# Attention, 2D-FFT mixing and an FFN on one core: VectorE's order tied to the first batch's transform, that transform by row chunks, W2's Gram products later, fewer unused products

## The chip, the cores and the metric
One core of one Trainium2 chip runs the program alone. The metric is the device time of one execution in microseconds (us). Every run of the kernel before gave between 1111.65 and 1112.94 us.

## What is computed
For each of 8 batches: windowed causal attention (8 heads, 576 positions, head size 64, window 128, a linear distance bias with a slope per head), its result `x` (576 x 512) mixed by a two-dimensional Fourier transform, normalised, and sent through a two-layer FFN. Cut to what matters:

```
scores = q @ k^T / 8 - slope[h] * (i - j)      where 0 <= i - j < 128
x      = softmax(scores) @ v                   # heads side by side: 576 x 512
u      = x + real(fft(fft(x, axis=seq), axis=model))
un     = (u - mean(u)) / sqrt(var(u) + 1e-6)
out    = u + relu(un @ W1) @ W2                # W1 512 x 2048, W2 2048 x 512
```

## The kernel before
**Pieces of work.** A batch's attention runs over four pairs of heads, numbered p = 4b + j. A pair has three groups of scores (`scores`, L370): q·k products on TensorE, a VectorE operation that adds the bias and reduces to the minimum (L399), ACT's exponential, then either a transpose on TensorE (`turn`, L423, batches 0 and 1, in f32) or f16 high and low parts and DMA transposes (`halves`, L406, the later batches). `values` (L435) multiplies by v, and `weigh` (L460) divides by the sums and writes the result into the tile X. In the trace an f32 product of scores or values shows as two records. After each group of scores of the first eight pairs, `busy` (L282) issues two 128x512 products whose result nobody reads.

**The transform** (`fourier`, L502) takes X in three chunks c of the sequence. `begin` (L505) clears one row. `fold_a`, `fold_b`, `fold_c`, `fold_d` (L513 to L557) add and subtract mirrored halves on VectorE and split them into f16 high (ACT) and low parts (VectorE). `rows(g)` (L559) multiplies the four column groups g by a cosine or sine table, nine products for each g over all three chunks; `rows_hi` (ACT) and `rows_lo` (VectorE) split the result. `cols(j)` (L591) is the second dimension, for three blocks of rows j; `cols_out` (ACT) brings it back, `cols_add` (VectorE) adds it to X: for j < 2 to X[j] and, mirrored, to X[2 + j]. `norm` (L656) takes two tiles: statistics (L669, L670), reciprocal deviation (L671 on VectorE, the power on GpSimd, L672), two scalings on ACT (L681, L682), a subtraction on VectorE (drawn at L155) and a DMA transpose on SP's queue into uT, which the FFN reads.

**The FFN** (`ffn`, L694): per two tiles, products with W1 (L707), relu on ACT (L712), its low part on VectorE (L155), products with W2 (L721), an addition, a store. Batches alternate 384 and 480 W1 products.

**The weights** (`weights`, L161) are made once, in 16 chunks of 512 columns: a load on SP's queue into one of four (W1) or three (W2) stages, `rebias` on ACT (L180), `join` on VectorE (L185, L186; the stage is then free), four Gram products on TensorE (`gram`, L192), from which `top_of` and `scale` take one scale; after it f16 high parts (`high`, ACT, L212) and low parts (`low`, VectorE, L215). W2's stages are the X buffers of batches not yet begun.

**What sets the order.** The program is written out by a list of times. `put(t, f)` (L151) pushes a piece of work with a time of the list, and the loop at L780 pops them in order; a framework then places instructions on each engine, with this order as their priority, by a model of when each is ready. On the chip every engine takes its instructions in that fixed order, SP's DMA queue too. Times of attention come from BEGIN and PACE, those of the transform from `put` calls at the end of `fourier` (L628 to L654), those of the FFN from FORWARD, those of the weights from the last lines (L778, L779).

## Time and profile before

| what | value |
|---|---|
| time, median of 3 runs | 1111.89 us (1111.65 to 1112.94) |
| profiled execution | 1110.7 us, span 1108.9 us |
| mean granted TensorE clock | 0.964 of full speed |
| TensorE busy | 1057.5 us, 95% |
| VectorE, ACT, GpSimd busy | 721.4, 570.1, 19.2 us |
| DMA share over the span (largest queue) | 34.2% |

Start times count from the span's first instruction. Products on TensorE are pipelined, so a busy time includes a tail that overlaps the next; where a price is wanted, the distance between starts is the better figure.

### The profile page before, as it was taken

Reading aid. Unit: us, or ns where it says so; the run is one execution under the profiler, and the core shown is the slowest. Engines: PE = TensorE matmul, PEld = TensorE weight load, DVE = VectorE, ACT = ScalarE, POOL = GpSimd, SP = SyncE. Lnnn points to the kernel's source line nnn. Section 1 sums busy time; section 2 is a strip of 40 time slices with the busy share of each in tenths; the row PEclk is TensorE's granted clock in tenths of the full one; section 3 lists DMA queues with packets and bytes.
Section 4 is the critical chain, followed back from the end, with each engine's and each line's share of the span. In section 5 each row is a group of like instructions: output and inputs, shape, how many; then the busy total and the mean of one; then the engine's idle time right before and its main releaser. Section 6 shows DMA issues by size and latency. Waiting matters only on the chain.

```text
span 1108.9 us, 23827 instructions
## 1 busy us (share of the span) xinstructions
PE 1057.5 (95%) x9252; PEld 739.8 (67%) x9252; DVE 721.4 (65%) x2255; ACT 570.1 (51%) x1330; POOL 19.2 (2%) x53
## 2 busy tenths in 40 slices
PE   7999898997999989999899999999999999999998
PEld 5776675765766657585658567675657667767665
DVE  4888689349768586979595868778575844362111
ACT  5887595337545376476654657375535531241000
POOL 0000000000000000000000000000000000000000
PEclk9995879998999999999899999999999999999999
DMA  9952042126432326335432364335422330020000
GB/s 359 362 170 65 13 92 68 49 48 123 104 83 54 95 56 139 88 74 117 103 89 60 70 111 95 77 70 100 113 77 40 68 70 1 20 48 20 20 11 20
DMA packets 178544, 95.35 MB, mean 86 GB/s; under 512 B 152960, under 2 KB 161152, under 8 KB 178432
## 3 DMA queue, kind: packets, MB, share of 16 engines
q1 hardware_dynamic: 177856, 92.39, 34.2%
q8 instruction: 72, 1.18, 0.4%
q10 hardware_dynamic: 576, 1.45, 0.3%
q14 instruction: 40, 0.33, 0.1%
HBM read 48.19 MB, written 9.44 MB: 52 GB/s over the span
## 4 chain that ended last, share of the span: by engine, by line
PE 67%; DVE 15%; DMA 7%; ACT 5%; issue 4%; SPq 1%; POOL 0%; DVEq 0%; ACTq 0%
PE fp L721 27%; PE fp L707 25%; PE sp L386 4%; PE pd L563 3%; DVE P L399 3%; DMA qr<-q_dram 3%; PE pv L447 2%; DMA pt<-P 2%; DVE P L155 2%; DVE hbuf L155 1%; DVE st L669 1%; PE sp L430 1%; DMA uT<-un 1%; ACT P L155 1%; DMA hbuf<-w_dram 1%
## 5 line engine op out<-in xcount | busy, mean ns | idle before, releaser
L721 PE MATMUL fp<-wall,hbuf 128*128 128x512 f16 x1728 | 391.5, 380 | 4.2 <-DVE hbuf L155 4.2
L707 PEld LDWEIGHTS <-wall 128*128 128x128 f16 x3840 | 343.7, 100 | 70.7 <-issue 14.1
L707 PE MATMUL fp<-uT,wall 128*128 128x256 f16 x3072 | 372.2, 278 | 17.1 <-DMA uT<-un 9.3
L721 PEld LDWEIGHTS <-hbuf 128*128 128x128 f16 x1728 | 164.0, 98 | 190.1 <-issue 7.9
L155 ACT ACTIVATE P<-P,nb 128x256 f32<-128x256 f32 x320 | 142.9, 479 | 78.3 <-DVE nb L399 76.4
L712 ACT ACTIVATE hbuf<-fp 128x512 f16<-128x512 f32 x144 | 84.8, 589 | 183.7 <-PE fp L707 183.4
L155 DVE SCALAR_TENSOR_TENSOR hbuf<-fp,hbuf 128x512 f16<-128x512 f32 x144 | 99.0, 688 | 113.3 <-ACT hbuf L712 112.4
L399 DVE CUSTOM_DVE_ANT_0 P<-sp,rg,nsl 128x256 f32<-128x256 f32 x240 | 98.4, 449 | 21.6 <-PE sp L386 11.0
L155 DVE SCALAR_TENSOR_TENSOR P<-P 128x256 f16<-128x256 f32 x240 | 88.7, 389 | 32.8 <-ACT P L412 31.7
L412 ACT ACTIVATE P<-P 128x256 f16<-128x256 f32 x240 | 86.5, 383 | 11.3 <-DMA pt<-P 5.0
L386 PE MATMUL sp<-kk,qq 64*128 64x256 f16 (+5 forms) x800 | 76.1, 280 | 2.2 <-ACT qq L361 1.2
L155 DVE SCALAR_TENSOR_TENSOR X<-fp,misc,X 128x512 f32<-128x512 f32 x32 | 23.7, 742 | 52.6 <-PE fp L721 52.6
L452 PE MATMUL pv<-vhs,pt 128*128 128x65 f16 x432 | 54.2, 195 | 0.3 <-DVE X L471 0.2
L455 PE MATMUL pv<-vl,pt 128*128 128x64 f16 x432 | 54.3, 193 | 0.0
L456 PE MATMUL pv<-vhs,pt 128*128 128x65 f16 x432 | 54.3, 194 | 0.0
L707 PE MATMUL fp<-wall,wall 128*128 128x128 f16 x768 | 47.5, 223 | 2.5 <-DVE hbuf L155 2.2
L452 PEld LDWEIGHTS <-pt 128*128 128x128 f16 x432 | 41.1, 98 | 8.4 <-issue 0.8
L455 PEld LDWEIGHTS <-pt 128*128 128x128 f16 x432 | 40.4, 99 | 7.8 <-issue 0.2
L386 PEld LDWEIGHTS <-qq 64*128 64x128 f16 (+1 forms) x720 | 30.8, 99 | 19.9 <-issue 14.8
L456 PEld LDWEIGHTS <-pt 128*128 128x128 f16 x432 | 40.5, 97 | 0.1
L563 PE MATMUL pd<-tab_sb,fh 128*128 128x289 f16 x174 | 39.7, 293 | 0.0
L546 ACT ACTIVATE fh<-abcd,sc 128x512 f16<-128x512 f32 (+1 forms) x24 | 17.3, 719 | 39.7 <-DVE abcd L538 39.7
(160 smaller groups left out, 1249.7 us busy)
## 6 DMA issues: line engine op xcount, KB each, us to landing
qr<-q_dram SPq DMA_DIRECT2D x28, 304.0 KB, 3.1
hbuf<-w_dram SPq DMA_DIRECT2D x16, 512.0 KB, 6.8
out_dram<-X SPq DMA_DIRECT2D x32, 256.0 KB, 2.2
vr<-v_dram SPq DMA_DIRECT2D x23, 320.0 KB, 3.1
kr<-k_dram SPq DMA_DIRECT2D x24, 289.0 KB, 3.0
X<-w_dram SPq DMA_DIRECT2D x11, 512.0 KB, 4.8
pt<-P SPq DMA_TRANSPOSE x240, 2.4
wall<-w_dram SPq DMA_DIRECT2D x5, 512.0 KB, 4.3
```

The costliest lines, as they stand in the source:

```text
L155: put(now[0] + dt, lambda: f(*a, **kw))
L386: T.matmul(sp[e][:m, col:col + n], qq[h, c0:c0 + m], keys(kk[h], ti), start=(x == 0), stop=(x == len(prods) - 1))
L399: V.tensor_tensor_reduce(pt[:m, 0:n], sp[e][:m, col:col + n], tab[:m, pc:pc + n], mul, 3.0e38, ALU.add, ALU.min, nb[:m, ti:ti + 1])
L412: A.activation(hi, P32, AF.Copy, scale=2.0 ** 14)
L447: T.matmul(pv[:, ti], pt[:, col:col + 128], ops[p][2][:, e, vc], start=first, stop=last)
L452: o = T.matmul(pv[:, ti], ph, vh[:, e, vc], start=first, stop=False)
L455: T.matmul(pv[:, ti, 0:D], ph, vl[:, e, vc], start=False, stop=False)
L456: T.matmul(pv[:, ti], pl, vh[:, e, vc], start=False, stop=last)
L563: T.matmul(zp[:, :NS], st["in", c][l][:m, g], tab1_sb[:m, (0 if g < 2 else 2) + t, c], start=(c == 0 and p == 0), stop=(c == 2 and p == 2))
L707: T.matmul(fp[:, i * n:(i + 1) * n], w1_ap(e, c, f0 + i), uT[:, j, c, 0:n], start=(c == 0 and p == 0), stop=(c == 3 and p == 2))
L712: A.activation(ht[:, 0], fp, AF.Relu)
L721: T.matmul(op, hh[f][:, a, i * 128:(i + 1) * 128], w2_ap(e, f), start=(f == 0 and p == 0), stop=(f == 15 and p == 2))
```

## The change
- `CHAIN = 0.15`; the first two times of FORWARD, at which the FFNs of batches 0 and 1 enter the list, go from 17.1 to 22 and from 39.6 to 41.6.
- `busy` issues its unused products for the first four pairs and not the first eight.
- W2's chunks are placed 0.4 instead of 0.5 apart, its high and low parts from 16.8 instead of 18.5, and all of its Gram products at one late time instead of one chunk behind each join.
- Batch 0's transform is no longer placed by times of its own: it is a list of steps, 0.15 apart. The row products go by chunk (`rows_of`: groups 0 to 2, chunk 2, then 0, then 1; group 3 whole), the mirrored addition into X[2 + j] is a step of its own, and the first two tiles are normalised before the third block of columns.
- While the list's time is below 25, every VectorE instruction gets an order dependency, without a semaphore, on the last VectorE instruction of that chain, so that VectorE's order is the list's there.
- `squares` of pairs above 9 is kept in program order, and it and the scales of those pairs are placed 0.6 or 0.7 later; the load of pair 8 is placed at 19.2.

```diff
+CHAIN = 0.15
...
-FORWARD = (17.1, 39.6, 64.7, 88.7, 112.7, 136.7, 160.7, 184.7, 208.7)
+FORWARD = (22, 41.6, 64.7, 88.7, 112.7, 136.7, 160.7, 184.7, 208.7)
...
+    def link(f, *a, **kw):
+        f(*a, **kw)
+        linked[0] = True
+
+    def place(b, t, f, *a, **kw):
+        if b == 0:
+            put(t, lambda: link(f, *a, **kw))
+        else:
+            put(t, lambda: f(*a, **kw))
...
-            put(t + 2 * dt - 0.3, gram, c)
+            put(t + 2 * dt - 0.3 if wi == 0 else t0 + 16.5 * dt, gram, c)
...
+        if p > 4 * NF + 1:
+            tc.keep_in_program_order(o)
...
-        for _ in range(SPIN if p < 8 else 0):
+        for _ in range(SPIN if p < 4 else 0):
...
+        def rows_of(gs, c):
+            for g in gs:
+                if c == 2:
+                    st["zp", g] = bank(b)
+                for p, (l, t) in enumerate(((0, 0), (1, 0), (0, 1))):
+                    T.matmul(st["zp", g][:, :NS], st["in", c][l][:KCH[c], g], tab1_sb[:KCH[c], (0 if g < 2 else 2) + t, c],
+                             start=(c == 2 and p == 0), stop=(c == 1 and p == 2))
...
+        if b == 0:
+            uTs[b] = []
+            pair = lambda i: lambda: st["X"][2 * i:2 * i + 2]
+            steps = [(begin, ), (fold_b, 2), (fold_c, 2), (fold_a, 0), (fold_b, 0), (fold_d, 2), (fold_c, 0),
+                     (rows_of, (0, 1, 2), 2), (fold_a, 1), (fold_b, 1), (fold_d, 0), (fold_c, 1), (rows_of, (0, 1, 2), 0),
+                     (fold_d, 1), (rows_of, (0, 1, 2), 1)]
+            for g in range(3):
+                steps += [(rows_hi, g), (rows_lo, g)]
+                if g == 0:
+                    steps += [(rows, 3)]
+            steps += [(rows_hi, 3), (rows_lo, 3), (middle, ), (middle_out, ), (cols, 1), (cols_out, 1), (cols, 0), (cols_add, 1), (mirrored, 1),
+                      (cols_out, 0), (cols_add, 0), (norm, b, pair(0), None), (cols, 2), (mirrored, 0), (cols_out, 2),
+                      (cols_add, 2), (norm, b, pair(1), None)]
+            for i, (g, *a) in enumerate(steps):
+                place(b, t0 + CHAIN * i, g, *a)
+            return
...
-            t0 -= 2.6 if p == 4 * NF else 2.9
+            t0 = 19.2 if p == 4 * NF else t0 - 2.9
...
-                put(t0 + 1.2 + 0.2 * x, squares, p, x)
+                put(t0 + (1.2 if late or p == 4 * NF else 1.8) + 0.2 * x, squares, p, x)
+            if p > 4 * NF + 1:
+                t0 += 0.7
...
-    weights(1, 9.5, 0.5, 18.5, 0.4)
+    weights(1, 9.5, 0.4, 16.8, 0.3)
+    traced, seen = nc.cur_bb.bb.instructions, 0
+    tied = {mybir.EngineType.DVE}
     while queue:
         now[0], _, f, a = heappop(queue)
+        linked[0] = False
         f(*a)
+        fresh = list(traced)[seen:]
+        seen += len(fresh)
+        for i in fresh:
+            e = i.engine
+            if e in tied and now[0] < 25:
+                if e in ties:
+                    tc.add_manual_dep(i, ties[e].name, mybir.DependencyInfo(
+                        mybir.DependencyClass.NoSync, mybir.DependencyReason.DATA), reason="order")
+                if linked[0]:
+                    ties[e] = i
```

What this does to the order is shown at two places. In the names below wall0 is W1; wall1 is the buffer of W2, and before W2 is in it, of batch 0's inputs; X_107 is one of W2's stages, X_321 batch 0's result. Numbers behind a name count the program's buffers.

TensorE just ahead of the first FFN product, before:

```order
L430 MATMUL sp1_2044<-ident_85,P_1941 128x128 x2
L140 MATMUL pd_1778<-sq_1711,misc_94 128x3
L447 MATMUL pv_1961<-vr_1430,pt_1690 128x65 x3
L447 MATMUL pv_1961<-vr_1430,pt_1800 128x65 x4
L447 MATMUL pv_1961<-vr_1430,pt_1908 128x65 x2
L140 MATMUL pd_2039<-m1_2037,misc_94 128x1
L447 MATMUL pv_2060<-vr_1758,pt_1955 128x65 x3
L447 MATMUL pv_2060<-vr_1758,pt_2012 128x65 x4
L707 LDWEIGHTS wall0_105
L707 MATMUL fp_1445<-uT_1320,wall0_105 128x256
```

and now, with the last of W2's Gram products (L208) close ahead of it:

```order
L208 LDWEIGHTS wall1_106
L208 MATMUL fp_1301<-wall1_106 128x128
L141 MATMUL pd_1391<-wm1_1389,misc_94 128x1
L446 MATMUL sp0_1488<-ident_85,P_1376 128x128 x2
L446 MATMUL sp1_1505<-ident_85,P_1379 128x128 x2
L757 LDWEIGHTS wall0_105
L757 MATMUL fp_1646<-uT_1266,wall0_105 128x256
```

The value products of batch 1's last two pairs (L447) stood ahead of the first FFN product and now stand behind it; counted over the whole order, 64 score products, 90 value products, 108 transposes and 24 unused products of attention precede it now, and 80, 133, 140 and 48 before. All 128 Gram products precede it in both.

VectorE at the end of batch 0's columns, before (L618 and L619 add columns to X, L669 is the statistics, L615 to L626 the third block of columns, L671 the deviation):

```order
L618 TENSOR_TENSOR X_321<-X_321,ds_1244 128x512
L619 TENSOR_TENSOR X_321<-X_321,ds_1244 128x512
L399 ISA P_1941,nb_1940<-sp1_1928,rel_sb_90 128x256
L399 ISA nb_1940 128x1
L399 ISA P_1943,nb_1940<-sp1_1928,rel_sb_90 96x256
L399 ISA nb_1940 96x1
L467 TENSOR_SCALAR ri_1923<-pv_1802 128x5
L669 BN_STATS st_1324<-X_321 128x6
L669 BN_STATS st_1327<-X_321 128x6
L399 ISA P_2000,nb_1999<-sp0_1993,rel_sb_90 128x256
L399 ISA nb_1999 128x1
L615 TENSOR_TENSOR ds_1312<-ab_1289 33x257
```

and now (L642 is the former L618, L657 the mirrored addition, L717 the statistics, L719 the deviation, L162 the subtraction of `norm`; L199 and L200 are a join of W2):

```order
L642 TENSOR_TENSOR X_321<-X_321,ds_1254 128x512
L200 SCALAR_TENSOR_TENSOR wall1_106<-wall1_106 128x512
L717 BN_STATS st_1270<-X_321 128x6
L718 BN_AGGR ag_1267<-st_1270 128x2
L717 BN_STATS st_1273<-X_321 128x6
L199 TENSOR_SCALAR wall1_106<-wall1_106 128x512
L718 BN_AGGR ag_1267<-st_1273 128x2
L200 SCALAR_TENSOR_TENSOR wall1_106<-X_107,wall1_106 128x512
L719 TENSOR_SCALAR rstd_1268<-ag_1267 128x2
L724 SCALAR_TENSOR_TENSOR nmr_1269<-ag_1267,rstd_1268 128x2
L162 TENSOR_TENSOR un_1283<-un_1283 128x512
L657 TENSOR_TENSOR X_321<-X_321,ds_1254 128x512
```

Batch 1's score reductions have gone from between the steps, joins of W2 have come, and the third block's additions stand behind the first two tiles' statistics. From `begin` to the deviation VectorE has 13 joins, 8 W1 low parts, 10 score reductions and one `weigh` beside the chain's own rows; before, 2 or 3 joins, 6 low parts, 26 reductions and 5 `weigh`. Ahead of `begin` stand 19 joins, 48 reductions and no W1 low part; before, 29 or 30, 54 and 2. Between batch 0's and batch 1's first FFN products the totals ahead of each mark meet again: at batch 1's first one 174 score products and 261 value products precede it now, 170 and 246 before.

## Rows read from the trace of the kernel before

**Rows 1.** the page's busy times (us, share of the span, instructions) and clock by 40 slices

```profile
PE 1057.5 (95%) x9252; PEld 739.8 (67%) x9252; DVE 721.4 (65%) x2255; ACT 570.1 (51%) x1330; POOL 19.2 (2%) x53
...
PEclk9995879998999999999899999999999999999999
```

**Rows 2.** windows between the marks: length, busy time of each engine, granted clock, DMA share, GB/s

```profile
5.50:78.00 72.50, 70.55 (x540) 52.63 (x540) 54.36 (x201) 55.55 (x118) 0.00 (x0) 1.00 0.86 311
78.00:147.00 69.00, 60.63 (x356) 47.01 (x355) 54.14 (x180) 48.91 (x110) 2.02 (x5) 0.69 0.23 60
147.00:267.00 120.00, 109.27 (x900) 74.46 (x899) 80.45 (x235) 62.48 (x144) 1.92 (x5) 0.96 0.29 63
267.00:1109.00 842.00, 817.03 (x7462) 565.68 (x7460) 532.40 (x1641) 401.01 (x958) 14.37 (x34) 0.98 0.32 71
```

**Rows 3.** windows around the clock's first fall

```profile
45.00:62.00 17.00, 17.00 (x143) 13.40 (x142) 15.58 (x53) 14.66 (x31) 0.00 (x0) 1.00 0.68 235
...
80.00:90.00 10.00, 7.91 (x52) 5.73 (x52) 10.00 (x30) 9.18 (x21) 0.00 (x0) 0.87 0.63 179
90.00:100.00 10.00, 10.00 (x43) 7.90 (x42) 10.00 (x31) 5.60 (x11) 0.10 (x1) 0.50 0.01 2
```

**Rows 4.** timeline of VectorE at the transform's beginning: start, length, engine, line, output<-input

```profile
79.87 0.48 DVE L511 MEMSET X<- 1x512 f32 x1
...
80.89 0.67 DVE L186 SCALAR_TENSOR_TENSOR wall<-X,wall 128x512 int32<-128x512 int32 x1
81.49 0.41 DVE L399 CUSTOM_DVE_ANT_0 P<-sp,rel_sb 128x256 f32<-128x256 f32 x1
```

**Rows 5.** timeline of TensorE at the two first FFN products

```profile
146.54 1.67 PE L707 MATMUL fp<-uT,wall 128*128 128x256 f16 x7 [1.43 <-DMA uT<-un]
...
266.73 3.59 PE L707 MATMUL fp<-uT,wall 128*128 128x256 f16 x16 [6.45 <-DMA uT<-un]
```

**Rows 6.** timeline of TensorE in batch 0's attention

```profile
42.78 2.32 PE L284 MATMUL fp<-tab_sb 128*128 128x512 f16 x10
44.94 0.39 PE L194 MATMUL fp<-wall 128*128 128x128 bf16 x4
...
67.15 2.17 PE L447 MATMUL pv<-wall,pt 128*128 128x65 f32 x18
69.25 1.14 PE L386 MATMUL sp<-kk,qq 64*128 64x256 f32 x8
70.33 0.40 PE L194 MATMUL fp<-wall 128*128 128x128 bf16 x4
70.57 0.50 PE L430 MATMUL sp<-ident,P 128*128 128x128 f32 x3
70.90 0.39 PE L194 MATMUL fp<-wall 128*128 128x128 bf16 x4
...
72.41 2.22 PE L447 MATMUL pv<-wall,pt 128*128 128x65 f32 x18
```

**Rows 7.** groups of VectorE by shape, 80 to 141 us: busy, mean ns, idle before

```profile
L215 DVE SCALAR_TENSOR_TENSOR wall<-wall,misc 128x1024 f16<-128x1024 f32 x6 | 7.6, 1269 | 0.0
...
L572 DVE SCALAR_TENSOR_TENSOR zl<-fp,zh 128x289 f16<-128x289 f32 x3 | 1.4, 462 | 7.8 <-ACT zh L568 7.8
...
L467 DVE TENSOR_SCALAR ri<-pv 128x5 f32<-128x5 f32 x6 | 0.9, 156 | 3.1 <-PE pv L447 3.1
...
L615 DVE TENSOR_TENSOR ds<-ab 128x257 f32<-128x257 f32 x2 | 0.9, 428 | 1.2 <-ACT ab L609 1.2
```

**Rows 8.** timeline of VectorE at batch 0's first deviation

```profile
136.57 0.16 DVE L671 TENSOR_SCALAR rstd<-ag 128x2 f32<-128x2 f32 x1
```

**Rows 9.** waits, 146 to 267 us: engine and line, what for, us, times, longest

```profile
PE fp L707 <- DMA uT<-un: 7.9, 2, 6.4
...
PE pd L140 <- ACT wall L251: 3.5, 1, 3.5
```

**Rows 10.** the page's DMA issues: KB each, us to landing

```profile
X<-w_dram SPq DMA_DIRECT2D x11, 512.0 KB, 4.8
```

More of the change, by code (lines that the diff above doesn't have):

```diff
@@ L155, in after @@
         put(now[0] + dt, lambda: f(*a, **kw))
+    ties = {}
+    linked = [False]
+    def link(f, *a, **kw):
[6 more added lines that the diff above has]
+            put(t, lambda: f(*a, **kw))
     stage = xp.tile([128, 5, DM], F32, name="X").rearrange("p a b -> p (a b)")
@@ L250, in squares @@
             raw = raw.rearrange("p a b c -> p (a b c)")
-        A.activation(junk[:, 0:n[x]], raw, AF.Square, accum_out=sq[b, 0][:, j, x:x + 1])
+        o = A.activation(junk[:, 0:n[x]], raw, AF.Square, accum_out=sq[b, 0][:, j, x:x + 1])
+        if p > 4 * NF + 1:
+            tc.keep_in_program_order(o)
     def pair_sums(p):
@@ L618, in cols_add @@
                 V.tensor_tensor(X[j], X[j], ds[:, 0:512], ALU.add)
-                V.tensor_tensor(X[2 + j], X[2 + j], ds[:, 512:0:-1], ALU.add)
+                if b == 0:
+                    st["ds", j] = ds
+                else:
+                    V.tensor_tensor(X[2 + j], X[2 + j], ds[:, 512:0:-1], ALU.add)
             else:
@@ L626, in cols_add, with mirrored @@
                 V.tensor_tensor(ut[p0 + 64:p0 + 96], X2[64:96], ds[64:96, 0:512], ALU.add)
+        def mirrored(j):
+            X, ds = st["X"], st["ds", j]
+            V.tensor_tensor(X[2 + j], X[2 + j], ds[:, 512:0:-1], ALU.add)
+        if b == 0:
+            uTs[b] = []
[13 more added lines that the diff above has]
+            return
@@ L628, in fourier @@
         f = STRETCH[b]
-        put(t0, begin)
+        place(b, t0, begin)
         for c, t in ((2, 0.0), (0, 0.8), (1, 1.5)):
             if c < 2:
-                put(t0 + f * (0.1 + 0.7 * c), fold_a, c)
-            put(t0 + f * t, fold_b, c)
-            put(t0 + f * (t + 0.5), fold_c, c)
-            put(t0 + f * (t + 0.8), fold_d, c)
+                place(b, t0 + f * (0.1 + 0.7 * c), fold_a, c)
+            place(b, t0 + f * t, fold_b, c)
+            place(b, t0 + f * (t + 0.5), fold_c, c)
+            place(b, t0 + f * (t + 0.8), fold_d, c)
@@ L636, in fourier @@
         t = t0 + f * 2.6
         for g in range(4):
-            put(t, rows, g)
-            put(t + f * 0.3, rows_hi, g)
-            put(t + f * 0.5, rows_lo, g)
+            place(b, t, rows, g)
+            place(b, t + f * 0.3, rows_hi, g)
+            place(b, t + f * 0.5, rows_lo, g)
             t += f * 0.75
-        put(t, middle)
-        put(t + f * 0.2, middle_out)
+        place(b, t, middle)
+        place(b, t + f * 0.2, middle_out)
         t += f * 0.55
         for j in (1, 0, 2):
-            put(t, cols, j)
-            put(t + f * 0.25, cols_out, j)
-            put(t + f * 0.6, cols_add, j)
+            place(b, t, cols, j)
+            place(b, t + f * 0.25, cols_out, j)
+            place(b, t + f * 0.6, cols_add, j)
@@ L651, in fourier @@
         for i, t1 in enumerate((t - f * 0.1, t + f * 0.7)):
-            put(t1, norm, b, lambda i=i: st["X"][2 * i:2 * i + 2], t + f * (0.9 + 1.6 * i))
+            place(b, t1, norm, b, lambda i=i: st["X"][2 * i:2 * i + 2], t + f * (0.9 + 1.6 * i))
         if b % 2 == 1:
-            put(t + 1.5, norm, b, lambda: [st["ut"]], t + 4.1)
+            place(b, t + 1.5, norm, b, lambda: [st["ut"]], t + 4.1)
     def norm(b, of, t1):
@@ L673, in norm @@
         f = min(STRETCH[b], 1)
-        put(t1 - 0.5 * f, lambda: V.scalar_tensor_tensor(nmr[:, :n], ag[:, :n, 0], -1.0, rstd[:, :n], ALU.mult, ALU.mult))
+        if t1 is None:
+            f, t1 = 0.2, now[0] + 0.2
+        place(b, t1 - 0.5 * f, lambda: V.scalar_tensor_tensor(nmr[:, :n], ag[:, :n, 0], -1.0, rstd[:, :n], ALU.mult, ALU.mult))
         uns = {}
@@ L682, in scaled @@
             A.activation(both[:, 0:512], tiles[i], AF.Identity, scale=s, bias=o)
-            after(0.3 * f, V.tensor_tensor, both[:, 512:1024], un, both[:, 0:512], ALU.subtract)
+            place(b, now[0] + 0.3 * f, V.tensor_tensor, both[:, 512:1024], un, both[:, 0:512], ALU.subtract)
             dst = uT[:, :, :, i * 128:(i + 1) * 128].rearrange("p e c t -> p (e c) t")
-            after(0.5 * f, nc.sync.dma_start_transpose, dst, both)
+            place(b, now[0] + 0.5 * f, nc.sync.dma_start_transpose, dst, both)
         for i in range(n):
-            put(t1 + f * (0.8 * i - 0.3), scaled, i)
+            place(b, t1 + f * (0.8 * i - 0.3), scaled, i)
     ov = out.rearrange("(t p) d -> t p d", p=128)
```

## The prediction, made before the change was run

> **What bounds the kernel now.** I read the page's engine totals first: TensorE is busy for 95% of the span, no other engine for more than 65% [rows 1]. So the time is TensorE's work, the idle time between its products, and what its clock takes. The slices of the granted clock show where it takes something: it is 0.8 or more everywhere but in slices 4 and 6, and full or nearly so behind slice 10 [rows 1]. Then I cut the span at the events that the edits touch [rows 2]. Until 78 us (batch 0's attention) TensorE is busy 70.6 of 72.5 us at clock 1.00, so fewer products there mean less time. From 78 to 147 (batch 0's transform and normalisation, with batch 1's attention beside it) it is busy 60.6 of 69 at a mean clock of 0.69; this stretch ends when the first FFN product has its operand, so it is set by a chain of dependent steps, not by TensorE. Afterwards the FFNs fill TensorE: 109.3 of 120 us, then 817.0 of 842. The last stretch has only 25 us of idle time in all; what reaches it is mostly the date at which it starts. Finer windows show the clock's fall: 7.9 of 10 us busy from 80 to 90, and 0.50 right behind, though TensorE is then busy without a gap [rows 3].
>
> Four marks divide the program, and I price each stretch by itself: batch 0's transform begins at 79.87 [rows 4], the first FFN product of batch 0 starts at 146.54 and that of batch 1 at 266.73 [rows 5], and the rest.
>
> **Stretch A, until the transform begins.** Three things go. (1) 24 of 48 unused 128x512 products: ten of them take from 42.78 to 44.94 [rows 6], 0.216 us each, so 24 x 0.216 = 5.2 us. (2) W2's first 44 Gram products, which now come after batch 0's attention: four take 0.24 us (70.33 to 70.57) [rows 6], so 44 x 0.06 = 2.6 us. Both sums count in full only where TensorE has no gap, which [rows 2] nearly grants. (3) The last value product ends at 74.63 (72.41 + 2.22) [rows 6], yet the transform's first VectorE instruction starts 5.2 us later [rows 4], behind joins, score reductions and a W1 low part in VectorE's queue. The order now has 10 joins, 6 score reductions and 2 W1 low parts fewer ahead of it. What has to stand there (reading the sums, a reciprocal, a 320-element product) takes about 1.3 us, so I take 4.0 off. Against these I put back 1.4: VectorE is itself busy 54.4 of 72.5 us here [rows 2], and a product that goes often uncovers a wait. Sum -10.4 (bounds -4, if TensorE merely waits for VectorE instead, and -12.5): the transform begins at 69.5.
>
> **Stretch B, transform to first FFN product (66.7 us now).** With the ties, VectorE's rows from the beginning to batch 0's reciprocal deviation are one fixed list, and their sum is a floor. A start follows the one before it a little sooner than its duration says: a join's second instruction takes 0.67 but the next starts after 0.60, a score reduction 0.41 and 0.35 [rows 4]. So I take 1.19 for a W1 low part (mean 1.27, [rows 7]) and 0.94 for a join's two instructions. The list now has 8 W1 low parts (9.5 us), 13 joins (12.2), 10 score reductions (3.2), one weighing (0.7) and the transform's own rows up to the first two tiles' statistics (about 17.0): 42.6 us. Before, 26 score reductions and 5 weighings stood there, but only 2 or 3 joins, and the rows of the third column block as well. Waits come on top. Before, VectorE waited 7.8 us for the rows' high parts, 3.1 for value products and 1.2 for the columns [rows 7]; the second kind has all but gone, the joins now fill part of the first, and rows taken chunk by chunk leave only the last chunk's products behind the last fold. Between 0 and 12 I take 5, nearer to the low end. The tail from that deviation to the first product took 9.97 us (136.57 to 146.54) [rows 5, 8]; it keeps its steps (power, two scalings, subtractions, transposes), and I leave it at 10.0. Four loads of v no longer stand ahead of the transposes in SP's queue, two of W2's loads now do; I set that at nothing within a bound of 1 us. 42.6 + 5 + 10 = 57.6, so -9.1: first product at 127.1, 19.4 earlier than now.
>
> **Stretch C, first product of batch 0 to first product of batch 1 (120.2 us now).** The order shows that TensorE reaches the first FFN product with 16 score products, 43 value products and some 36 transposes of batch 1 fewer behind it; they now lie among batch 0's FFN, where TensorE is the bound, and have to be paid. By [rows 6] a value product costs 0.233 us (nine, two records each, from 67.15 to 69.25), a transpose 0.11 (three in 0.33), a 256-wide score product 0.27 (eight records in 1.08) to 0.53: 10.0 + 4.0 + 4.3 to 8.5, so 18.3 to 22.5. I take 21.5, near the upper end, since the moved scores stand tile by tile and not interleaved. Against that, batch 1's FFN waited for its transposed operand (6.4 us, the longest of the two such waits that make 7.9) and a small sum for ACT's squares (3.5) [rows 9]. Between batch 1's last column products and its first FFN product TensorE now has 13.2 us of other products (by the order, at full-clock prices) instead of 7.1, which covers the 6.4, and the squares' load is issued earlier, which covers the 3.5. The opening at half clock stays. 21.5 - 6.4 - 3.5 = +11.6: batch 1's first product at 127.1 + 120.2 + 11.6 = 258.9, 7.8 earlier.
>
> **Stretch D, the rest.** The counts of products ahead of each later mark are the same within a few; squares are pinned to their order and moved by 0.6 or 0.7 of the list's time. Nothing there should move: 0, bounds -3 and +3 out of the 25 us of idle time [rows 2].
>
> **Sum.** -10.4 - 9.1 + 11.6 = -7.9 us on the profiled execution's own 1110.7 us (span 1108.9 and 1.8 around it): 1102.8. The median of the shown runs is 1.2 above that execution: 1104.0. It is the same as saying: 5.2 us of unused products are gone for good, and some 2.7 of TensorE's idle and half-clock time with them; the rest of the 19.4 is only moved.
>
> **A rule against it.** TensorE's granted clock fell to 0.50 after a stretch in which it was busy 7.9 of 10 us, and was 1.00 from 45 to 62, where it was busy 17.00 of 17 us and had no unused products at all, the last one being over by 44.94 [rows 3, 6]. So the sum has no term for the clock. The Trainium skill's page "TensorE: Matmul & The Clock Gate", section "HAM oscillation — how this bites in real kernels", says that idle gaps between products make the chip lower TensorE's clock, and that each such gap is paid for again in slow products. By that rule, taking filler products away between 10 and 45 us invites just such gaps, and the sum would get the second rival's term; the fall at 80 to 90 agrees with it, the unfilled 45 to 62 shows a stretch where it had nothing to bite on.
>
> **Rivals.**
> - *VectorE's fixed order waits for loads: slower.* Thirteen joins of W2 now stand at fixed places inside the chain. A stage is free again only after its join, and there are three: load (4.8 us to landing, [rows 10]), issue 0.5, ACT 0.6 and join 0.9 make 6.8 us per round of three, against 3 x 42.6/13 = 9.8 us that the list gives. Above a landing time of about 7.8 us each further microsecond costs 13/3 = 4.3 us, and everything behind waits, the first FFN product included. At 10.6 us: +12, 1116. For it: the same transfers run beside a full DMA share of 0.86 before 78 us; against: that share is 0.23 after it [rows 2]. 0.09.
> - *The clock falls in batch 0's attention: slower.* If a gap there halves the clock over some 30 us, half of their products' work is paid twice: +15 to +20 on the forecast, about 1121. For: the fall in [rows 3]; against: the unfilled stretch at 1.00. 0.06.
> - *The gain is given back: no change.* In batch 0's FFN, VectorE (80 of 120 us busy) and ACT (62) [rows 2] get batch 1's moved reductions and exponentials besides the hidden layer; if the two waits of stretch C stay (9.9 us), the sum is about +2: 1111 to 1113. 0.09.
> - *More than forecast.* If the shorter chain has so few gaps that the half-clock opening of the FFN goes as well, or waits in B are 0, another 5 to 10 us go: 1094 to 1099. 0.20.
>
> That the edits don't take effect is excluded by the program order, which has them.
>
> **How the numbers follow.** The forecast itself has 0.56. With the rival of more gain: faster 0.76. A run can tell 0.2% (2.2 us) from no change. Same 0.09, slower 0.09 + 0.06 = 0.15. The forecast's own bounds (A +6/-2, B +7/-5, D 3 either way, not all at once) make some 1098 to 1109; with most of the larger gain below, and the given-back case above, the range is 1095 to 1113, which leaves out the two slower rivals and the far end of the gain.
>
> **What will show it.** Right: 24 records of unused products; granted clock 1.00 until 70; transform at 69 to 71; first FFN product near 127 (120 to 136) with VectorE's waits for W2's joins between the marks below 5 us; batch 1's first product near 259 and no long wait for its operand; the distance from there to the end as before within 3 us. Wrong: a first FFN product behind 140 (first rival), a clock below 1.00 before 70 (second), or a first product at 127 with batch 1's still at 265 (third).

## The result and the profile after

The changed kernel took 1078.54 us (median of 4 runs, 1077.12 to 1080.65) against 1112.41 for the kernel before beside it: ratio 0.9697, 95% interval 0.9677 to 0.9717. The forecast was 1104.0 with a low end of 1095.0. The direction was right and the size was not: 33.9 us went, more than four times the 7.9 of the sum. Shown below is one execution with a span of 1075.8 us. Executions that took over 1.5% longer than the fastest of the same kernel, at a lower granted clock, are left out of all ratios.

The page's busy times and its clock by slices:

```profile
PE 1032.0 (96%) x9228; PEld 720.4 (67%) x9228; DVE 721.9 (67%) x2255; ACT 567.5 (53%) x1330; POOL 19.2 (2%) x53
...
PEclk9987799999999999999999999999999999999999
```

The same four stretches as in [rows 2], with their new limits, by windows (length, busy time of each engine, granted clock, DMA share, GB/s):

```profile
5.50:64.00 58.50, 57.24 (x452) 44.07 (x452) 41.29 (x167) 46.55 (x105) 0.00 (x0) 1.00 0.83 308
64.00:117.30 53.30, 35.28 (x265) 25.54 (x261) 48.60 (x122) 39.16 (x82) 1.00 (x4) 0.69 0.49 144
117.30:248.50 131.20, 128.75 (x1073) 90.47 (x1074) 102.64 (x335) 81.97 (x187) 3.83 (x7) 0.98 0.31 66
248.50:1075.80 827.30, 810.64 (x7443) 560.12 (x7443) 529.34 (x1633) 397.57 (x955) 13.50 (x33) 0.99 0.33 72
```

The marks in the timelines of VectorE and TensorE (start, length, engine, line, operation): the last value product of batch 0, the transform's beginning, the first deviation, the two first FFN products.

```profile
61.42 2.17 PE L463 MATMUL pv<-wall,pt 128*128 128x65 f32 x18
...
64.71 0.48 DVE L527 MEMSET X<- 1x512 f32 x1 [0.16 <-DVE X L487]
...
109.61 0.16 DVE L719 TENSOR_SCALAR rstd<-ag 128x2 f32<-128x2 f32 x1
...
117.32 2.95 PE L757 MATMUL fp<-uT,wall 128*128 128x256 f16 x13 [0.33 <-DMA uT<-un]
...
248.47 1.48 PE L757 MATMUL fp<-uT,wall 128*128 128x256 f16 x12 [0.71 <-DMA uT<-un]
```

| stretch | before, us | forecast | after | change: forecast, measured |
|---|---|---|---|---|
| A, to the transform's beginning | 79.9 | 69.5 | 64.7 | -10.4, -15.2 |
| B, to batch 0's first FFN product | 66.7 | 57.6 | 52.6 | -9.1, -14.1 |
| C, to batch 1's first FFN product | 120.2 | 131.8 | 131.2 | +11.6, +11.0 |
| D, to the end of the span | 842.2 | 842.2 | 827.4 | 0, -14.8 |

The same 33.1 us by kind. TensorE's idle time in the span fell from 51.4 us (1108.9 - 1057.5, [rows 1]) to 43.8 (1075.8 - 1032.0): -7.6. The clock took (1 - 0.964) x 1108.9 = 39.9 us of full-speed time before and (1 - 0.977) x 1075.8 = 24.7 after: -15.2. The 24 unused products and, as shown below, the score products are shorter by 5.0 and 3.3. These make 31.1; 2 us stay without a name. This is an estimate, since idle time at half clock counts in both of the first two terms, but it says that nearly half of the gain is clock that was not lost, a term that the sum did not have. In stretch D alone the clock is at half for some 25 us in six stretches before and for 10 us in three in the change (the last 3 us of the span left out), and each of the nine begins in an idle gap of TensorE or shortly behind one.

### The profile page after: what moved, and what is told of

Same layout as the page of the kernel before. It is cut to its first block, busy times and chain, and to the rows that moved or that the text cites. A ratio compares the mean times of both kernels' runs of the same rounds, so it can differ in the third digit from the quotient of the medians.

```text
span 1075.8 us, 23753 instructions
## 1 busy us (share of the span) xinstructions
PE 1032.0 (96%) x9228; PEld 720.4 (67%) x9228; DVE 721.9 (67%) x2255; ACT 567.5 (53%) x1330; POOL 19.2 (2%) x53
## 4 chain that ended last, share of the span: by engine, by line
PE 73%; DVE 13%; ACT 6%; DMA 4%; issue 3%; SPq 1%; POOL 0%; ACTq 0%; DVEq 0%
PE fp L771 30%; PE fp L757 27%; PE sp L402 4%; PE pd L579 3%; PE pv L463 2%; DVE P L415 2%; DVE P L156 1%; PE pd L621 1%; DMA pt<-P 1%; PE pv L468 1%; DMA qr<-q_dram 1%; PE sp L446 1%; ACT P L156 1%; PE pv L472 1%; DVE st L717 1%
## 5 line engine op out<-in xcount | busy, mean ns | idle before, releaser
L757 PEld LDWEIGHTS <-wall 128*128 128x128 f16 x3840 | 338.4, 99 | 55.3 <-issue 10.5
L757 PE MATMUL fp<-uT,wall 128*128 128x256 f16 x3072 | 367.2, 275 | 4.1 <-DVE hbuf L156 2.2
L156 ACT ACTIVATE P<-P,nb 128x256 f32<-128x256 f32 x320 | 140.7, 478 | 111.3 <-DVE nb L415 109.8
L402 PE MATMUL sp<-kk,qq 64*128 64x256 f16 (+5 forms) x800 | 71.2, 278 | 5.2 <-ACT qq L377 2.2
L562 ACT ACTIVATE fh<-abcd,sc 128x512 f16<-128x512 f32 (+1 forms) x24 | 17.2, 718 | 39.6 <-DVE abcd L554 39.6
L731 ACT ACTIVATE un<-X,nmr,rstd 128x512 f32<-128x512 f32 x32 | 25.8, 805 | 22.3 <-DVE nmr L724 22.3
```

The lines of the kernel that those rows point to most:

```text
L156: put(now[0] + dt, lambda: f(*a, **kw))
L402: T.matmul(sp[e][:m, col:col + n], qq[h, c0:c0 + m], keys(kk[h], ti), start=(x == 0), stop=(x == len(prods) - 1))
L731: A.activation(un, tiles[i], AF.Identity, scale=s, bias=o)
L757: T.matmul(fp[:, i * n:(i + 1) * n], w1_ap(e, c, f0 + i), uT[:, j, c, 0:n], start=(c == 0 and p == 0), stop=(c == 3 and p == 2))
```

## The experiments

The changed kernel is called the change. Undoing runs edit the change, "alone" runs edit the kernel before. Ratios are to the kernel before on the same chip, with 95% intervals; the change itself has 0.9697, and 0.9695 (0.9682 to 0.9708) when it ran again beside the last run. On the chips of these runs the kernel before took between 1108.7 and 1121.2 us (medians 1112.9 to 1116.2), so a few microseconds between runs on different chips say little where their ratios don't differ. A cost in microseconds is the run's median less 1078.5.

### The last stretch: the squares

**Squares undone.**

```diff
-        if p > 4 * NF + 1:
-            tc.keep_in_program_order(o)
...
-            t0 = 19.2 if p == 4 * NF else t0 - 2.9
+            t0 -= 2.6 if p == 4 * NF else 2.9
...
-                put(t0 + (1.2 if late or p == 4 * NF else 1.8) + 0.2 * x, squares, p, x)
-            if p > 4 * NF + 1:
-                t0 += 0.7
+                put(t0 + 1.2 + 0.2 * x, squares, p, x)
```

> The changed kernel, with the squares of the later pairs free again and at their old times, and pair 8's load at its old time. Theory 1: the 14.9 us that the last stretch (from batch 1's first FFN product to the end) gave come from ACT no longer standing at a square whose load is still out. Then the first FFN products stay at 117 and 248 us, the last stretch is back at 842 us (827 in the changed kernel), the gaps ahead of FFN products in it are back at some 20 us, and the time is about 1093. Rival 2: the last stretch gained because batch 2 and the later ones start earlier relative to their own loads and transforms (from the shift of the first two FFNs). Then the last stretch stays at 827 and the time at 1078.5.

Measured: 1085.31 us, 0.9754 (0.9725 to 0.9782). The first FFN products stood at 118.8 and 251.1, the last stretch took 834.3: +7, half of what the first theory expected for that stretch.

**Squares alone.** The same diff the other way, on the kernel before.

> The kernel before with nothing but the later squares: pinned in program order, they and the scales 0.6 to 0.7 later in the list, pair 8's load at 19.2. Theory 1: they are worth 7 us in the last stretch, as undoing them cost, whatever stands before: its 842 us become about 835, the time about 1105, the first two FFN products stay at 146 and 267 us. Rival 2: they carry the whole gain of that stretch, of which the undoing saw half because batch 0's and 1's new order had moved the loads too: 827, time about 1097.

Measured: 1101.60 us, 0.9887 (0.985 to 0.9924), the first FFN products at 149.2 and 269.1, the last stretch 830.7. The gain of 12.6 us (8 to 17) lies between the two theories, and in the stretch they named.

**The pin alone, and the later place alone.** On the kernel before, the first run adds

```diff
+        if p > 4 * NF + 1:
+            tc.keep_in_program_order(o)
```

and the second the other lines of that diff.

> The kernel before with the squares of pairs above 9 kept in program order, nothing placed later. Theory 1: ACT stands at a square because the scheduler's model thinks its load done and draws it ahead of work that is ready; the pin stops that, ACT's waits for q's load fall from 32.6 us to near 14, and the last stretch gives most of its 11 us: about 1102. Rival 2: in program order they are as early as before, ACT's waits stay at about 30 us, and the time stays within 3 of 1113.

> The kernel before with the squares and scales of those pairs 0.6 to 0.7 later in the list and pair 8's load at 19.2, without the pin. Theory 1 (the pin does it): the scheduler draws them forward all the same, the waits for q's load stay near 30 us, the time within 3 of 1113. Rival 2 (the place does it): the waits fall to near 14 us and the time to about 1102.

Measured: the pin 1102.40 us, 0.9871 (0.9803 to 0.9939); the later place 1109.85, 0.9953 (0.9922 to 0.9983). ACT's waits at the squares in the last stretch (engine and line, what for, us, times, longest), first before, then in the change, with the pin alone, with the place alone:

```profile
ACT wall L251 <- DMA qr<-q_dram: 32.6, 17, 6.0
```

```profile
ACT wall L265 <- DMA qr<-q_dram: 13.7, 4, 6.1
```

```profile
ACT wall L251 <- DMA qr<-q_dram: 6.0, 4, 4.3
```

```profile
ACT wall L251 <- DMA qr<-q_dram: 36.5, 17, 5.5
```

ACT used to stand 17 times in front of a square whose load of q was still out, and everything behind it on ACT stood too. The same wait with the squares undone in the change, and with pin and place together, alone on the kernel before:

```profile
ACT wall L265 <- DMA qr<-q_dram: 32.9, 18, 4.2
```

```profile
ACT wall L251 <- DMA qr<-q_dram: 10.8, 3, 5.2
```

What TensorE waited for in the last stretch, before and in the change:

```profile
PE fp L707 <- DVE hbuf L155: 10.1, 6, 4.0
PE fp L721 <- DVE hbuf L155: 3.5, 4, 1.3
```

```profile
PE fp L757 <- DVE hbuf L156: 3.5, 4, 1.3
...
PE fp L771 <- DVE hbuf L156: 0.9, 1, 0.9
```

and with the pin alone:

```profile
PE fp L709 <- DVE hbuf L155: 8.1, 8, 3.5
```

So the pin takes ACT's waits away and the later place by itself does not, and by the medians the pin carries the larger part of the gain; since the two intervals touch, a split in microseconds is not to be had. How the gain gets from ACT to the end is shown only in part. The last stretch by windows, with the squares undone in the change and with pin and place together alone:

```profile
251.10:1085.40 834.30, 807.47 (x7445) 559.30 (x7443) 530.05 (x1636) 399.38 (x955) 13.49 (x33) 1.00 0.33 72
```

```profile
269.10:1099.80 830.70, 813.50 (x7462) 562.64 (x7462) 528.36 (x1636) 399.45 (x956) 13.85 (x33) 0.99 0.33 72
```

Undone, TensorE idles there for 26.8 us (834.30 - 807.47) where the change has 16.7, though its clock is fuller; alone, it idles for 17.2 where the kernel before has 25.0. So the two together work through TensorE's idle time. TensorE's waits for the hidden layer's low parts fell from 10.1 to 3.5 us in the change, and stayed at 8.1 with the pin alone, whose last stretch of 835.2 (7 less) came with a higher mean clock, 0.969 for 0.964, at nearly the same idle time. Since the kernel before itself ran at 0.957 to 0.968 on that chip, how the pin alone gains stays open.

### The unused products

**All 48 again.**

```diff
-        for _ in range(SPIN if p < 4 else 0):
+        for _ in range(SPIN if p < 8 else 0):
```

> The changed kernel with 48 unused products as before. Theory 1: TensorE is full there, so the 24 products cost 0.216 us each again: +5.2 us, 1083.7, the transform beginning 5 us later. Rival 2: since the attention of batch 0 now waits at other things (TensorE idles 6.7 us until 80 where it idled 1.9), part of them is hidden: +2 to +3 us. Rival 3: they hold the granted clock up in the transform behind them: no change or a little less time.

Measured: 1089.09 us, 0.9786 (0.9755 to 0.9818): +10.5, twice the first theory. Batch 0's last value product comes 9.0 us later than in the change (72.4 against 63.3), the transform begins at 73.8. The time from one start to the next, added up per kind until that product, explains it: the 24 products take 5.2 us more, and the score products, 100 records for 96, 3.2 more. Timelines of TensorE show why, first of the kernel before:

```profile
34.49 0.92 PE L386 MATMUL sp<-wall,qq 64*128 64x256 f32 x6
35.34 0.41 PE L194 MATMUL fp<-wall 128*128 128x128 bf16 x4
35.68 0.49 PE L386 MATMUL sp<-wall,qq 64*128 64x128 f32 x2
36.09 0.38 PE L140 MATMUL pd<-m,misc 128*128 128x1 f32 x2
```

and of the change:

```profile
32.53 0.92 PE L402 MATMUL sp<-wall,qq 64*128 64x256 f32 x8
33.39 0.40 PE L208 MATMUL fp<-wall 128*128 128x128 bf16 x4
```

Both show the same group of scores, four records 256 wide and four 128 wide, under the form of the first. In the kernel before six of them take 0.85 us (34.49 to 35.34), and the last two, behind Gram products, another 0.41; in the change all eight take 0.86 (32.53 to 33.39). The two heads of a pair sit in the two halves of the 128 rows; where their products stand next to each other, the trace has them start about 0.01 us apart and run side by side. Before, other products stood between them more often. That this order is the cause is read from such rows; no run changed it alone. Nor is all of the 3.2 us that: the four records more are batch 1's, moved ahead of the mark, and batch 0's own 80 take only 0.7 us more. These 80 take 18.1 us in the kernel before, 16.1 in the change and 17.1 with 24 unused products fewer and nothing else, so the unused products are not all that parts them.

**24 fewer, alone.** That diff the other way, on the kernel before.

> The kernel before with 24 unused products fewer and nothing else. Theory 1: beside 24 x 0.216 = 5.2 us, the score products of two heads stand next to each other more often, which took 3.2 us off them in the comparison of the two traces; the last value product of batch 0 comes 8 us earlier, the transform begins near 71, and since the transform's order is the old one, 5 to 8 us reach the end: 1104 to 1107. Rival 2: the waits come back as gaps and the gain is under 3 us. Rival 3: only 5.2 us go at the last value product, and the score products cost what they did.

Measured: 1098.28 us, 0.9859 (0.9817 to 0.99). No theory held: 15.7 us (11 to 20). The profiled execution is 12.1 us shorter than that of the kernel before. The transform begins at 76.0 and the first FFN products stand at 142.1 and 254.6, so 4.4 us are gone at batch 0's first product; 7.7 more go in stretch C (112.5 in place of 120.2) and none behind. The longest waits of stretch C, [rows 9], shrank there: the small sum's 3.5 us are gone, and the longest wait for the operand is 4.8 in place of 6.4,

```profile
PE fp L707 <- DMA uT<-un: 9.5, 2, 4.8
```

and the half clock around batch 0's first FFN product lasts 13.7 us in place of 20.5. How fewer unused products before 45 us bring this about was not followed.

**None, and 12.** On the change, the first run with 0 and the second with 2:

```diff
-        for _ in range(SPIN if p < 4 else 0):
+        for _ in range(SPIN if p < 2 else 0):
```

> The changed kernel without any unused product. Theory 1: the remaining 24 take 6.6 us of TensorE in batch 0's attention (0.27 each in the trace of the changed kernel), and it has only 1 us of gaps there: 5 to 7 us go, 1072 to 1074. Rival 2: they stand where TensorE would wait for loads anyway (until about 30 us): 0 to -2. Rival 3: they hold the clock up at the beginning; the granted clock falls below 1.00 before 60 us and the time grows by 5 or more.

> The changed kernel with unused products behind the first two pairs' scores only, 12 in place of 24. Theory 1: with none the granted clock was at half from 13 to 51 us, with 24 it stayed full; what counts are the products in the first 20 us, where TensorE waits for loads and has little else, so with 12 the clock stays up, the transform begins 2.5 to 3 us earlier, and the time is 1075 to 1077. Rival 2: the clock falls once the products end: half from some 20 or 30 us on, the transform begins at 75 or later, 1086 to 1094.

Measured: none, 1093.39 us (three executions; a fourth took 1111.47), 0.9826 (0.9779 to 0.9873); 12 of them, 1079.91, 0.9684 (0.9642 to 0.9726), which is the change's own time. Windows of the kernel with none:

```profile
5.50:13.00 7.50, 5.63 (x38) 3.94 (x38) 3.19 (x17) 3.79 (x8) 0.00 (x0) 1.00 1.02 394
13.00:51.00 38.00, 38.00 (x180) 29.76 (x177) 15.34 (x71) 20.15 (x46) 0.00 (x0) 0.51 0.65 241
```

and of the one with 12:

```profile
5.50:13.00 7.50, 6.25 (x40) 3.96 (x41) 3.04 (x15) 3.77 (x8) 0.00 (x0) 1.00 1.03 398
13.00:51.00 38.00, 37.38 (x305) 28.93 (x305) 28.77 (x120) 34.32 (x79) 0.00 (x0) 1.00 0.99 367
```

With none, the clock is at its lower level from 13 to 51 us, 180 products go through in that window where 305 do with 12, and the transform begins at 79.9. That is the third rival of the expectation, and the prediction's second, at another number of products. By the Trainium skill, page "TensorE: Matmul & The Clock Gate", section "HAM oscillation — how this bites in real kernels", gaps between products bring the lower clock; the trace agrees in so far as the fall comes right behind a window with 5.6 of 7.5 us busy (6.25 with 12 products). Once down, it stayed down for 38 us in which the row shows TensorE busy without a gap. The 12 and the 24 both keep it up. The 12 that are gone save 3.2 us, but up to batch 0's last value product the scores take 2.4 us more (100 records for 96) and the transposes 0.9, so that product comes at 63.9 for 63.3.

### The ties

```diff
-    tied = {mybir.EngineType.DVE}
+    tied = set()
```

> The changed kernel without the order dependencies; by the program order VectorE then has 27 joins, 50 reductions and 2 W1 low parts ahead of the transform, and 30 reductions and 3 joins between it and the first deviation, nearly as before. Theory 1: this order is what gave stretches A and B; the transform begins at about 72 (79.9 less the 7.8 of the products that are gone), the first FFN product comes at about 136 (transform to product back at some 64), and about half of these 19 us reaches the end, since attention moves back ahead of the FFN: 1086 to 1090. Rival 2: the steps written as a list, rows by chunk, shorten the chain by themselves: transform to first product 53 to 56, time within 4 us of 1078.5.

Measured: 1097.39 us, 0.9857 (0.9817 to 0.9897): +19, more than either theory. The transform begins at 80.2 and the first FFN product comes at 161.6. Windows of that kernel:

```profile
5.50:67.00 61.50, 56.24 (x432) 42.09 (x432) 43.82 (x169) 46.60 (x103) 0.00 (x0) 1.00 0.93 344
67.00:143.00 76.00, 71.80 (x316) 53.84 (x317) 45.31 (x140) 43.91 (x97) 0.20 (x2) 0.51 0.20 58
```

From 67 to 143 TensorE is busy 71.8 of 76 us at clock 0.51. More of batch 1's attention goes ahead of the first FFN product again (108 records of its value products for 36 in the change, 82 of its scores for 48), and at half speed. The next run shows that the 19 us are not the price of this order alone.

**Ties and FFN times undone.** The edit above, and

```diff
-FORWARD = (22, 41.6, 64.7, 88.7, 112.7, 136.7, 160.7, 184.7, 208.7)
+FORWARD = (17.1, 39.6, 64.7, 88.7, 112.7, 136.7, 160.7, 184.7, 208.7)
```

> The changed kernel without the ties and with the old FFN times. Without the ties alone the first FFN product came at 162 us, 15 us later than in the kernel before, with 75 us of half clock ahead of it. Theory 1: the later FFN times suit only a transform that ends early: put back together with the old order of VectorE they make that loss, and with the old times it goes: first product at 140 to 146, time 1085 to 1088, as with the two small edits alone. Rival 2: the loss is the ties' alone (the list of steps 0.15 apart without them lets every other piece of work in between): first product at 155 or later, 1095 or more.

Measured: no comparison. Of four executions one took 1084.44 us (mean clock 0.976, first FFN product at 141.0) and three 1101 to 1108 (clock 0.954 to 0.957). The one at 1084 is what the first theory gave, the others the second; it stays open. The trace of that one can be laid beside the run with only the ties undone: ahead of the first FFN product both have the same 856 matrix products in the same order. The second window of above, here:

```profile
67.00:143.00 76.00, 64.46 (x434) 50.84 (x435) 63.90 (x213) 57.29 (x124) 1.70 (x5) 0.75 0.26 73
```

The clock falls at 67.6 us in both, is back at 95 here and only at 143 there, and the same products end 20 us earlier. What brought it back is not shown. So a good part of the ties' 19 us is a stretch of half clock that this order does not always have, and what the ties are worth without it is not known.

### The list of steps and the Gram products

**Steps by their old times.** The ties stay.

```diff
-        if b == 0:
-            uTs[b] = []
...
-            for i, (g, *a) in enumerate(steps):
-                place(b, t0 + CHAIN * i, g, *a)
-            return
...
-                if b == 0:
-                    st["ds", j] = ds
-                else:
-                    V.tensor_tensor(X[2 + j], X[2 + j], ds[:, 512:0:-1], ALU.add)
+                V.tensor_tensor(X[2 + j], X[2 + j], ds[:, 512:0:-1], ALU.add)
```

> The changed kernel with batch 0's transform written by its old times (rows by group, mirrored addition with the rest, norm of the first tiles behind the third block of columns), the ties kept on that chain. Theory 1: the transform begins at 65 as in the changed kernel; the chain to the first deviation is longer by the third block's columns (five additions of 0.3 to 0.7, some products at half clock, a wait for ACT), 5 to 7 us, and the rows' last groups come later by 2 to 3: first product at 125, time +4 to +8, about 1084. Rival 2: TensorE's time is the bound and the first FFN product's date only moves attention: +0 to +2.

Measured: 1081.06 us, 0.9713 (0.9685 to 0.9741). The first FFN product stands at 122.4, 5 us later, where the first theory had 8, and the intervals overlap: at most some 6 us of the total, perhaps nothing.

**W2's Gram products behind each join.**

```diff
-            put(t + 2 * dt - 0.3 if wi == 0 else t0 + 16.5 * dt, gram, c)
+            put(t + 2 * dt - 0.3, gram, c)
```

> The changed kernel with W2's Gram products behind each join again. Theory 1: 44 of them return to batch 0's attention at 0.06 us, 2.6 us, and cut the score products' runs apart for another 0.5 to 1; in exchange as many leave the transform's stretch, where TensorE idles: the transform begins 3 us later, the first FFN product 3, the end 2 to 4: 1081. Rival 2: TensorE's queue hits joins that are not done yet, and the transform is late by more than 5.

Measured: 1085.49 us, 0.9727 (0.9686 to 0.9768); beginning at 67.6, first FFN product at 123.3, 3 and 6 us later than in the change. Again between nothing and some 9 us at the end. Only 12 of the products, and not 44, came back ahead of batch 0's last value product (0.8 us); the scores, with the same 96 records, took 2.8 us more (21.0 for 18.2), which is most of the 3.

### The FFN times

**Old times.** The second diff of the section on the ties, with the ties in place.

> The changed kernel with the old times at which the FFNs of batches 0 and 1 enter the list. Theory 1: the part of the last stretch's 14.9 us that the squares don't carry (8 us) comes from here: that stretch is 835, the time about 1086. Rival 2: the times only set where batch 1's attention and the FFN mix, the last stretch stays at 827, and the total is 1078 to 1081.

Measured: 1093.83 us, 0.9828 (0.9783 to 0.9874). Both theories fall: it costs 15 us, and not in the last stretch (823.5). The first FFN product stays at 117.2, batch 1's comes at 267.3. TensorE's waits there, 150 to 270 us:

```profile
PE sp L402 <- ACT qq L377: 9.6, 1, 9.6
PE pd L141 <- ACT wall L265: 5.8, 1, 5.8
```

and the window of that wait:

```profile
250.00:268.00 18.00, 4.96 (x51) 3.61 (x52) 16.52 (x58) 12.03 (x25) 2.42 (x3) 0.53 0.51 104
```

With the earlier times batch 0's FFN ends at 240.8, and the transposes that make batch 1's operand are issued only at 262.5. In between TensorE stands at a small sum and at scores of batch 2, which wait for ACT; it is busy 5 of 18 us and its clock falls. The later times are what turns the early first product into time.

**Later still.** Three runs, with 24 and 42.6, 26 and 43.6, 24 and 41.6; the first:

```diff
-FORWARD = (22, 41.6, 64.7, 88.7, 112.7, 136.7, 160.7, 184.7, 208.7)
+FORWARD = (24, 42.6, 64.7, 88.7, 112.7, 136.7, 160.7, 184.7, 208.7)
```

> The changed kernel with batch 0's FFN 2 and batch 1's FFN 1 later in the list (24 and 42.6). Theory 1: the old times (17.1 and 39.6) cost 15 us, because batch 0's FFN used up TensorE's work ahead of batch 1's transform, so that TensorE idled 19.9 us between 150 and 270 and its clock fell; in the changed kernel only 3.1 us of idle time are left there, so nothing more is to be had: within 2 us of 1078.5. Rival 2: more of batch 1's attention ahead of batch 0's FFN brings batch 1's first product earlier still, 2 to 4 us, 1075. Rival 3: TensorE now idles in front of batch 0's FFN, +2 to +4.

> The changed kernel with batch 0's FFN at 26 and batch 1's at 43.6 in the list (22 and 41.6 in the change, 24 and 42.6 in the version that took 1073.8). Theory 1: the gain of the later times has its end where batch 0's FFN has too few of batch 1's products left to fill its own waits, or batch 1's transform is done before TensorE is free: within 2 us of 1073.8. Rival 2: it goes on, 1069 to 1071. Rival 3: TensorE idles in front of batch 0's FFN, 1077 or more.

> The changed kernel with batch 0's FFN at 24 in place of 22 and batch 1's time as in the change. Theory 1: batch 0's time carries the gain of the version with 24 and 42.6 (more of batch 1's attention runs ahead of the end of batch 0's FFN, so batch 2's transform and FFN find more of their inputs ready): 4 to 6 us below the changed kernel on the same chip. Rival 2: it needs batch 1's later time too, and alone the FFN of batch 1 comes before its operand: no change or up to 4 us more.

Measured: 1073.77 us, 0.9625 (0.959 to 0.9659); 1078.18, 0.9657 (0.9605 to 0.9708); 1075.71, 0.9674 (0.9659 to 0.9689), with the change at 1078.39 beside it. The first is the fastest kernel of this study: its whole interval lies below that of the change, on another chip. At 26 and 43.6 batch 1's first product slips to 262.2; by its time the gain is gone, by its ratio half of it, and its interval touches both others, so this is not settled. Batch 0's time alone gives 2.7 us, with intervals that still touch.

### Two edits alone

The kernel before with the squares' whole diff (as added by the change) and

```diff
-        for _ in range(SPIN if p < 8 else 0):
+        for _ in range(SPIN if p < 4 else 0):
```

> The kernel before with two edits alone: 24 unused products fewer and the later squares. Theory 1: the two act in different stretches (until batch 1's first product; behind it), so their gains add: 15.7 + 12.6 = 28, 1085, with the last stretch near 829. Rival 2: both remove the same gaps of the last stretch and of batch 1's start, and together they give 20 or less: 1092 or more.

Measured: 1085.95 us, 0.9752 (0.9704 to 0.9799). The gains add, as the first theory had it: 28 (22 to 33) of the change's 34 us come from these two, without any tie, list of steps or moved FFN. The order work on batch 0 gives the rest, some 6 us, and only as a whole: taking away its FFN times alone costs 15 us and its ties alone 19, more than all of it gives.

## Why the prediction was wrong

- **"Nothing there should move: 0, bounds -3 and +3"** (stretch D) is the step that failed most: -14.8. It took the squares for a displacement and judged by TensorE's product counts. The runs show that ACT stood 17 times, 32.6 us in all, at squares whose load of q was out, that the pin removes these waits, and that the squares are worth 7 us of this stretch (undone in the change) to 11.5 (alone). TensorE idles less in it (16.7 us for 25.0, from the windows) and its clock falls less ([rows 2]: 0.98, now 0.99). The other 3 to 8 us of the stretch belong to no single edit. The bound of 25 us of idle time was there; that ACT stood at those loads was in the trace of the kernel before, and was not used.
- **"Against these I put back 1.4"** (stretch A) had the wrong sign. The unused products and the Gram products are right (5.0 and 2.7 measured, 5.2 and 2.6 forecast), as is the queue behind the last value product: from 63.6 to 64.7, 1.1 us where 1.3 was put. What was missing is the score products' time, 3.3 us less: 1.9 of it is batch 0's own 80 records, whose two heads stand together more often, the rest batch 1's, 16 records ahead of the mark for 18.
- **"Between 0 and 12 I take 5"** and **the tail at 10.0** (stretch B): from the beginning to the deviation it took 44.9 us with VectorE busy for 43.0, so 2 us of waits; the tail from 109.61 to 117.32 took 7.7, with no other work between its scalings on ACT or ahead of its transposes in SP's queue. The floor of 42.6 was right to 0.4 (with the 0.35 that it reads for a reduction it would be 42.9).
- **Stretch C** was right, +11.0 for +11.6, and for its reasons: TensorE is busy there for 19.5 us more (128.75 for 109.27) where 21.5 was put, and idle for 8.3 less where 9.9 was put; the wait for batch 1's operand is down to 0.7 us, and no wait for the squares is left there. The 36 moved transposes are 32 by the counts in the section on the change, 0.4 us less. The run with the old FFN times shows that the moved times belong to this term: without them the stretch would have been 150 us. The sum took them in through the order, without naming them.
- **"So the sum has no term for the clock"** is the other large miss: some 15 of the 33 us by kind are clock. The second rival asked only whether it falls more; it falls less. Fewer gaps fit that, but no run separates the two. The reading of the slices left out where the loss was: they are not full behind slice 10, slice 20 is at 0.8 [rows 1]. What that rival feared is real, at none instead of 24.
- Of the rivals, the loads of W2 behind the ties did not bite: VectorE waited for their first ACT step 1.3 us in two places. "More than forecast" was the right side with too small a price, 5 to 10 where 25 came, and its conditions hold only in part: 2 us of waits are left in B, and the FFN still opens at half clock. The price of "the gain is given back" was added wrongly: its +2 is 1114 and not 1111 to 1113.

## What to carry to other kernels

Ask for each in-order engine what stands behind an instruction that waits for a load: a cheap one that stands too early holds everything behind it, and product counts on the busiest engine don't show it. When a stretch has idle time and half clock, look at both: here the stretches of half clock began in gaps or right behind them, and fewer gaps came with less half clock. An early result is worth only what the list lets TensorE do with it: move the consumer's due time along with the chain, and try it on both sides.

## What was not expected of the hardware

Products that use 64 of the 128 rows cost less side by side with those of the other 64: one group of scores took 0.86 us whole and 0.85 + 0.41 with a break in it. With no unused products the clock fell at 13 us and stayed at half for 38 us of uninterrupted products, most of them f32, while 12 fillers at the beginning kept it full. And with the same 856 matrix products in the same order ahead of the first FFN product, the half clock that began at 67.6 us lasted 27 us in one execution (ties and FFN times undone) and 75 in another (ties undone).
